# Casting the state powers to bf16 by transfers that GpSimd begins, with a new order of all steps, in a gated mix of attention and a state-space convolution

## The chip, the core and the metric

The kernel runs on one core of a Trainium2 chip. The metric is the device time of one execution in microseconds (us); smaller is better. The core's engines run side by side and meet at semaphores: PE (TensorE) multiplies matrices into PSUM, ACT (ScalarE) and DVE (VectorE) do the elementwise work and copy results out of PSUM ("evictions"), GpSimd (POOL) and SP (SyncE) begin transfers. Each engine runs its instructions strictly in the order in which they were written, so an instruction that waits holds up all that stand behind it on its engine.

## What is computed

Over 2048 tokens of width 512 the result is a gated sum of two branches, `g*a + (1-g)*b` with `g` a sigmoid of a weighted row sum of the input. Branch `a` is attention with 32 heads in four segments of 512 tokens, with a memory carried from segment to segment. Branch `b` is a state-space layer: each of the 512 channels has 128 complex states, whose powers give a long filter `K`, and the input is convolved with it.

```python
logdA = dt * A                                          # 512 x 128, complex
P = jnp.exp(logdA[:, :, None] * l[None, None, :])       # powers, l = 0 .. 2047 (rounded to bf16)
K = jnp.einsum('dn,dnl,dn->dl', Cc, P, dB).real
...
y = irfft(rfft(u padded) * rfft(K padded))[:L] + u * Dskip
...
return g * a + (1 - g) * b
```

## The kernel before

**How the order comes about.** `build_graph` makes a list of some 1800 steps, each with an engine, what it reads and writes, and a function that issues its instruction. Most evictions (`evac`, L223 to L229) and the cast of the powers are steps of the kind "ANY": they may run on ACT or on DVE. `ORDER` is a long text that a search outside the kernel has found; each word is a step's number, an `a` or `v` that puts a free step on ACT or DVE, and the buffer slots that it takes. `replay` reads it and so fixes the order on every engine; `emit` writes the instructions engine by engine and adds the semaphore waits that the data ask for. Transfers take their semaphores from a ring of 120 (`NDMA`): the 121st waits for the first to have landed. When SP has issued its last transfer it waits for all 120 in a row (L330 to L332).

**The stages.** To about 12 us parameters are loaded and transposed. The branches then run interleaved. *Attention*: for each of 4 segments and 4 head groups there are projections (L972 to L995), scores with an exponential of 128x2048 on ACT (L1062), masks (L1074), products with the values, and normalisations (L1034 to L1037). *Filter*: the states are squared nine times (below), tables of powers are multiplied up out of the results (L1157, L1160, L1164, all on DVE, for four blocks `c` of 128 channels), and PE correlates the tables ("lag" steps) into the filter. *Convolution*: two halves of 16 steps each, from about 130 us on, in which PE makes a spectrum X of the input, one K of the filter, DVE multiplies them (Y, L1266), PE turns the product back (V), and transfers on SP's queue load constants (`c_DNM`) and move parts. A last run on PE joins both branches and the output leaves in eight transfers.

**The state powers.** The channels are in two halves `h`. `Z` is an f32 tile of 128x512, 256 columns of real parts and 256 of imaginary parts. `ssm_powers` (L778) makes ten powers per half: ACT squares `Z` (L788), DVE makes the next `Z` of it (L789, L790). Of every `Z` a bf16 tile `pw` is made for the tables, in which each block of 128 channels has four strips of 128 columns: real, real again, imaginary, minus imaginary. For it there are three steps:

```python
# L796 on ACT or L797 on DVE: real and imaginary, cast to bf16
src = lambda Z=Z: ap(Z, 0, [[128, 2], [256, 2], [1, 128]])
dst = lambda pw=pw: ap(pw, 0, [[512, 2], [256, 2], [1, 128]])
# L798 on DVE: minus imaginary;  L800 on DVE: real again
```

So there are 20 casts (15 of them on DVE, 5 on ACT in this order), 20 negations and 20 copies. Table step `c` uses power 0 to 3 first, as copies into the table, and then all ten as factors; half 0 feeds blocks 0 and 1, half 1 feeds blocks 2 and 3. A table step waits for the whole `pw` of its power. GpSimd has only five memsets (L862, L914) and begins no transfer; SP begins all 263.

Of the kernel before, what the change touches and what calls it, by code (L numbers as in the profile page):

```python
# [7 lines left out]
ACT = mybir.ActivationFunctionType  # L8
# [4 lines left out]
NDMA = 120  # L13
# [80 lines left out]
class Op:  # L94
    __slots__ = ("eng", "cost", "fn", "deps", "key", "tiles", "wt", "seq", "alld", "tag", "alts", "isdma",
                 "idx", "inc", "val", "sem", "know", "waits", "pos")


class Sched:
# [61 lines left out]
    def op(self, eng, cost, fn, r=(), w=(), pw=(), key=None, acq=(), alts=None, isdma=False):  # L161
        o = Op()
        o.alts = alts
        o.isdma = isdma
        o.eng, o.cost, o.fn = eng, cost, fn
# [97 lines left out]
    def emit(self):  # L263
        nc, es = self.nc, self.es
        sems = {e: es.enter_context(nc.semaphore("q_" + e)) for e in ("PE", "ACT", "DVE", "POOL")}
        dsem = [es.enter_context(nc.semaphore("d%d" % i)) for i in range(NDMA)]
        block = es.enter_context(nc.Block())
        duse = [None] * NDMA
        dcnt = [0] * NDMA
        nd = 0  # L270
        last = {e: {} for e in self.prog}
        for o in self.order:
            know = dict(last[o.eng])
            o.waits = []
            deps = {id(d): d for d in o.alld}
            if o.isdma:
                k = nd % NDMA
                nd += 1
                if duse[k] is not None:
                    deps[id(duse[k])] = duse[k]  # L280
                duse[k] = o
                dcnt[k] += 1
                o.sem, o.val = ("D", k), dcnt[k]
            else:
                o.sem, o.val = o.eng, o.idx
# [28 lines left out]
        def make(e):  # L314
            def run(eng):
                for o in self.prog[e]:
                    need = {}
                    for d in o.waits:
                        s, v = tok(d)
# [9 lines left out]
                if e == "SP":  # L329
                    for k in range(NDMA):  # L330
                        if dcnt[k]:
                            eng.wait_ge(dsem[k], 16 * dcnt[k])  # L332
# [27 lines left out]
205/1 9/0 15/0 29/0 10/2 0/0 23/4/1 24v 54/0 1/0 57/1 30/11 38/5 33/9 21/0 39/0 14/1 31/2 17/0 34 35 36 32/6 45/1 37/7  # L360
44/12 58v/0 11/3 40/4 41 12/0 42 46/3 55/6 43 50/10 48/2 49/8 25/3/0 47 56v 51/1 52/0 61/3 3/0 59/0 60 16/0 53 62v/9
73/5 26a 178/1 74a/1 200/0/0/2 203/4/2 71/1 65/2 13/4 27/2/2 201a 72 173/7 202 63 85/4 83/3 84 18/0 20/0 204a 219/0/0
220 214/1/0/0 189/0 95/0 66/6 28v 67 250/3/2/0 174/1 96/0 98v/0 79/2 7/0 799/0 1247/1 208/2 221 97 64 86v/2 176/2 215
209a 99 109/3 190 87 175/0 240/0/1 241 588/0 1226/0 107/3 206/0 210/2 242 177 77/0 207a 994v/0 110v/3 75 181/1 179/2
76 191 111 108 88 228/0/2 251a 229 377/0 995v 122v/4 121/4 217 196/0 212/3 230 213v 119/3 78 197/0 223/0/3 224
1250/3/0 211a 89/0 120 123 998v/0 100 996v 192/0 225 253/2/0 1000/1 252 997v 254a 1002 222/0 999 1003/0 1001 124 1005
1004 236/0/0 237 134a/8 91/5 112 216 131/3 1232/2/1 226 135 1008 238 132/3 1233v 133 296/1/1 1011 1009/0 227 198/0
1248/2 1006/1 262/0/3 263 90 1249a 146v/5 231 6/0 1251a 235/2 199/0 232/0 1010 800/3 801 264 1234/3 136 147 145/7 233
1015/0 22/0 1252 234/1 103/0 101/3 1014 102 1235a 143/0 266/0/2 144 267 1016 1227/0/0 1007 1017 1012/0 158v/7 297a
193/0 148 1229/3 239 243 255/1/1/1 268 1230a 271/0/0 272 159 1236 113/3 1228a 273 378/3 244 293/0/1/1 279/0/1 280 1026  # L370
245/1 114/4 1231 294a 379 115 246 1013 391/0 247 1018/1 256 337/3/2 265/0 257 281 1242/2/1 1243a 1244/1 1245a 283/0/3
160 284 1246 1027/0 1019 269 270 274 589/2 155/0 285 157/1 156 295 218/1/0 125/3 802 380 275/2 1021/1 338a 307/0/2 308
127/3 590 258 1258/2/0 278/3 282 2/0 309 259 1020 1029 1259a 167a/6 592/0 276 1028 312/0/0 313 1022 1260/2 286 314 287
168 277/0 260/0 169 1239/0/1 248/1 1261a 288/2 1023 1240a 4/0 1024/0 1025 1030/1 303/0/1 304 126 1032 289 249a/0 305
334/0/0/2 1033/0 290 1034 139/7 335a 320/0/3 321 1035 1036/0 1031 298/2/0/1 137/0 306/0 310 339/1/1/0 1037 1237/3 311
315 322 1262 324/0/1 325 382/1 1238a 340 316/5 336 1043/3/0 1044 1045 341 1268/0 1265/1/0 138 299 300 317 151/1 326
318/1 182 1046 1241 301 194 1047v 149/0 291/2 346/0/2 292a 1266a 347 348 1038/2 1263/0 150 195 342 1039 1040 1041
1056v/0 1052v/0 1264a 319/1 1255/3/1 1061/1 350/0/0 351 383/0/2/0 323 327 328 1256a 161/1 1253/3 352 1055v 140v/9
355/0/3 1042a 1053v 1060 1054v 1289/1 1058/0 356 1057 386/2/0 1062 1254a 384a 1059 1066 1070/0 128v/0 398/3 1067/1 357
329/5 1063 349/0 1267 363/0/2 364 387a 353 1068 1069 1072 1048/0 8/0 385 330 399a 1071 92a/1 1073/1 1257 1064/0 1074  # L380
354 358 986/1 331 1079/1 1075 1065 359/4 1078 302/2 343 365 400/1/0/0 360 1080 344 401 443/3/1 361/0 402 93 1082/0
1081 367/0/1 1076/1 1083 444a 68a/4 368 1276/3/0 396/2 369 1274/1 405/0/0 1277a 1275a 1278 406 407 362/0 366 392/1
393a 397a 370 1284/3/1 1084 104v/3 129 1285a 371 409/0/3 410 1290/1/0 1292/2 1286/3 411 1293a 1077 372/5 1091/0 1085/1
1090 373 94 1086 374 1092 422/0/2 423 1087 445/1 1291a 1093 1094/0 1088/1 1095 1089 1294 394/2 390/1 440/1/1/1 424 261
395a 426/0/1 427 408/0 441a 1287a 442 116v/6 375/2 163/3 1271/1/0 412 162 446 170v/2 1288 490/3/0/2 428 1272a 413 491a
388/0 414/0/0 415 180 492 80v/7 152v/8 171 1101/1/1 1102 1103 1104 1269/3 416 459/0/3 376a 1105a 460 417 117 69 81 141
1281/2/1 421/1 105 425 429 430 164v/5 389 345 70 431/0 106 165 1270a 1279/3 418/3 432 1273 1049 1050 461 166 1282a
455/0/0 142 419 130 456 1096/2 1097 1098 1099 82 1280a 457 403 420/0 1302/3/0 1303a 433 118 448/0/1/1 449 153 1114v/0
1113v/0 1110v 1112v 1119/0 472/0/2 473 1300/1 1118 1111v 1116/1 1115 493/3/2 1283 1120 1117 474 1301a 1124 1121
464/0/1 1100a 465 1125/0 1128/1 450 1127 172 1126 1129 458/2 494a 1297/1/1 651/0/2/0 1295/3 462 463 1131/0 1304 466  # L390
476/0/0 1298a 1296a 477 652a 467 1307/1/0 471/3 475 332/0 478 520/0/3 1308a 521 1122/1 1130 1123 333a 1136 1132 468/3
522 1305/1 609/0/1 610a 1306a 512/0/2 1134/1 803 1137/0 381 513 469 1138 1133 434/0/2/0 470/1 1135 447/0 154 514
538/2/1/1 539a 479 503/0/1 504 541/2/0 505 451 480 495/0 1140/1 591 524/0/0 542a 435 1139 1106 1051 1323/0 436 1109
525 1141 1143/0 1148 540 481/3 437 484/0/5/1 482 1149/1 483 526 519/2 1309 1107 1299 1390/2 523 1108 1142 597/3/1 485
1150 486 507/0/3 1152/1 487 508 438/0 598a 1144 543/1 488/3 404/1/1 527 528 509 1145 1146/0 553/0/0 554 452 489a/0
439a 1151 602 506/3 510 511 453 546/0/1/1 529/0 515 1147 1310/1 530 1153 555 516/3 1337/1 1325/1 1326/1/2 547 653
531/0 496 1327a 1329 557/0/2 558 559 1328 1324/0 517 548 518 497/1 601/0 1154/1/0 1155 454 1156 549 593/0 498/0/0/0
# [1004 lines left out]
```

## Time and profile before

| | |
|---|---|
| median of 3 runs (lowest to highest) | 314.16 us (313.31 to 314.18) |
| the profiled execution, device time | 315.1 us |
| its span, first to last instruction | 313.3 us |
| mean granted clock of PE | 0.971 |
| busy: PE, DVE, ACT, GpSimd | 260.0, 264.3, 260.3, 3.2 us |
| chain of waits: DVE, PE, ACT, transfers | 31%, 30%, 20%, 9% |

The profile is one execution, recorded by the hardware. Its page gives busy times by engine, the span in 40 slices, transfers by queue, and groups of instructions: a line of the kernel, engine and operation, what is written and read, shape and number, then busy time, the mean duration of one in ns, and idle time of the engine before them with what ended it. "Busy time by stretches" gives the same for stretches of time. The "chain of waits" goes back from the last instruction, at each step to what released it or to the instruction before it on its engine; its pieces are given as start, length, engine and line. An engine's instructions overlap a little at their ends, so what one costs its engine is the distance from its start to the next one's start, not its duration.

### The profile page before, as it was taken

What the parts mean: (1) busy time and instruction counts of PE and PEld (TensorE: products, weight loads), DVE (VectorE), ACT (ScalarE), POOL (GpSimd) and SP (SyncE); (2) the same over time, 40 slices, a digit from 0 to 9 for tenths busy, and PEclk for the clock granted to TensorE, in tenths of its full rate; (3) what the DMA queues carried; (4) which work ended last, traced back from release to release, by engine and by line L of the source; (5) the groups of instructions that cost most, each with busy time, mean ns of one, the idle gap of its engine ahead of it and who ended that gap; (6) DMA issues with size and microseconds to landing.
All of it is one profiled execution on the core that took longest, in us unless ns stands there. A gap on an engine that the chain in (4) does not pass through costs nothing.

```text
span 313.3 us, 10366 instructions
## 1 busy us (share of the span) xinstructions
PE 260.0 (83%) x4393; PEld 183.1 (58%) x4430; DVE 264.3 (84%) x667; ACT 260.3 (83%) x315; POOL 3.2 (1%) x9
## 2 busy tenths in 40 slices
PE   1587688669977777989888899999999998999992
PEld 1343445345544543666546677667757775799892
DVE  1999999987999999999999768778999899883432
ACT  2899999997999999999999787988998998823250
POOL 2000000000000000000000000000000000000000
PEclk9999958996999999999999999999999999999999
DMA  5994111130402213431437676767668757873333
GB/s 148 273 235 84 35 68 50 36 104 10 144 33 71 79 47 106 108 97 25 130 112 237 191 216 180 228 187 254 204 191 245 249 164 238 242 250 91 109 112 100
DMA packets 49486, 44.51 MB, mean 142 GB/s; under 512 B 17184, under 2 KB 44832, under 8 KB 49440
## 3 DMA queue, kind: packets, MB, share of 16 engines
q1 hardware_dynamic: 49440, 43.85, 47.6%
q8 instruction: 35, 0.57, 0.8%
q14 instruction: 11, 0.09, 0.1%
HBM read 26.92 MB, written 6.29 MB: 106 GB/s over the span
## 4 chain that ended last, share of the span: by engine, by line
DVE 31%; PE 30%; ACT 20%; DMA 9%; issue 4%; SPq 4%; ACTq 0%; DVEq 0%
PE psum L680 29%; ACT sb L1062 9%; DVE sb L1157 7%; DMA sb<-c_DNM 7%; ACT sb L225 6%; DVE sb L1164 6%; DVE sb L1160 6%; SPq L221 4%; DVE sb L226 3%; ACT sb L788 2%; DMA sb<-sb 1%; DVE sb L1037 1%; DMA sb<-c_ident 1%; DVE sb L1266 1%; DVE sb L1034 1%
## 5 line engine op out<-in xcount | busy, mean ns | idle before, releaser
L680 PE MATMUL psum<-sb 128*128 128x17 bf16 (+12 forms) x4305 | 252.4, 224 | 39.1 <-ACT sb L1062 18.7
L680 PEld LDWEIGHTS psum<-sb 128*128 128x128 bf16 (+2 forms) x4342 | 176.6, 97 | 114.4 <-ACT sb L1062 32.2
L1062 ACT ACTIVATE sb<-psum 128x2048 bf16<-128x2048 f32 x80 | 152.4, 1905 | 5.4 <-PE psum L680 4.6
L225 ACT ACTIVATE sb<-psum 128x512 bf16<-128x512 f32 (+2 forms) x151 | 86.9, 627 | 25.4 <-PE psum L680 18.5
L226 DVE CAST sb<-psum 128x512 bf16<-128x512 f32 (+1 forms) x50 | 33.1, 677 | 5.1 <-PE psum L680 4.6
L1157 DVE TENSOR_TENSOR sb<-sb 128x512 bf16<-128x512 bf16 (+3 forms) x52 | 33.7, 663 | 0.0
L1164 DVE TENSOR_TENSOR sb<-sb 128x512 bf16<-128x512 bf16 (+3 forms) x52 | 33.5, 663 | 0.0
L1160 DVE TENSOR_TENSOR sb<-sb 128x512 bf16<-128x512 bf16 (+3 forms) x52 | 33.2, 656 | 0.0
L1266 DVE TENSOR_TENSOR sb<-sb 128x1024 bf16<-128x1024 bf16 x32 | 21.8, 688 | 6.9 <-DMA sb<-sb 5.5
L1074 DVE TENSOR_TENSOR sb<-sb 128x1024 bf16<-128x1024 bf16 (+1 forms) x40 | 22.8, 581 | 2.7 <-ACT sb L1062 2.7
L229 DVE TENSOR_SCALAR sb<-psum,sb 128x256 bf16<-128x256 f32 x18 | 8.5, 482 | 14.2 <-PE psum L680 9.4
L1037 DVE TENSOR_TENSOR sb<-psum,sb 128x256 bf16<-128x256 f32 x32 | 13.3, 420 | 0.6 <-PE psum L680 0.3
L228 ACT ACTIVATE sb<-psum,sb 128x256 bf16<-128x256 f32 x14 | 6.1, 473 | 6.8 <-PE psum L680 5.9
L788 ACT ACTIVATE sb<-sb 128x512 f32<-128x512 f32 x18 | 11.7, 653 | 0.0
L1034 DVE RECIPROCAL sb<-psum 128x16 f32<-128x16 f32 x32 | 8.1, 252 | 2.2 <-PE psum L680 2.1
L736 PE MATMUL psum<-sb 128*128 128x128 bf16 x24 | 3.1, 311 | 7.4 <-DMA sb<-c_ident 5.8
L226 DVE COPY sb<-psum 128x1024 bf16<-128x1024 bf16 x4 | 2.7, 686 | 6.8 <-PE psum L736 6.8
L1114 DVE TENSOR_TENSOR sb<-psum,sb 128x512 bf16<-128x512 f32 x12 | 8.2, 682 | 0.2
L993 ACT ACTIVATE sb<-sb 128x512 bf16<-128x512 bf16 x12 | 7.8, 652 | 0.0
L790 DVE SCALAR_TENSOR_TENSOR sb<-sb 128x256 f32<-128x256 f32 x18 | 7.4, 417 | 0.0
L789 DVE TENSOR_TENSOR sb<-sb 128x256 f32<-128x256 f32 x18 | 7.3, 414 | 0.1
L736 PEld LDWEIGHTS psum<-sb 128*128 128x128 bf16 x24 | 2.5, 144 | 8.2 <-DMA sb<-c_ident 5.8
(67 smaller groups left out, 109.7 us busy)
## 6 DMA issues: line engine op xcount, KB each, us to landing
sb<-c_DNM SPq DMA_DIRECT2D x32, 320.0 KB, 3.7
sb<-c_DNM SPq DMA_DIRECT2D x32, 192.0 KB, 3.1
scr_Z<-sb SPq DMA_DIRECT2D x16, 256.0 KB, 2.6
sb<-scr_Z SPq DMA_DIRECT2D x32, 128.0 KB, 3.0
sb<-sb SPq DMA_DIRECT2D x64, 64.0 KB, 3.2
sb<-sb SPq DMA_DIRECT2D x32, 128.0 KB
sb<-in_A_x_dram SPq DMA_DIRECT2D x5, 512.0 KB, 4.5
out_dram<-sb SPq DMA_DIRECT2D x8, 256.0 KB, 2.2
```

The lines of the kernel that those rows point to most:

```text
L221: return self.op(q, ("D", nbytes), lambda e: e.dma_start(out(), in_(), **kw), r=r, w=w, pw=pw, key=key, isdma=True)
L225: fa = lambda e: e.activation(dst(), src(), ACT.Copy)
L226: fd = lambda e: e.tensor_copy(dst(), src())
L680: mm = lambda e, o_, l, r_, st, sp, **kw: e.matmul(o_, lhsT=l, rhs=r_, start=st, stop=sp, skip_group_check=True, **kw)
L788: op("ACT", ("As", 512), lambda e, sq=sq, Z=Z: e.activation(ap(sq, n=512), ap(Z, n=512), ACT.Square), r=[Z], w=[sq], key=PW[h] + PWS * k)
L1037: op("DVE", ("V1", 256), lambda e: e.tensor_tensor(ap(o1, gi * 16, [[128, 4], [32, 4], [1, 16]]), ap(T, dims=[[68, 4], [17, 4], [1, 16]]), ...
L1062: o = op("ACT", ("Ax", 2048), lambda e, P=P, pT=pT: e.activation(ap(pT, n=2048), ap(P, n=2048), ACT.Exp, scale=0.25), r=[P], w=[pT])
L1074: op("DVE", ("V2", 128 * nb), lambda e, pT=pT, dims=dims: e.tensor_tensor(ap(pT, dims=dims + [[1, 128]]), ap(pT, dims=dims + [[1, 128]]), ...
L1157: op("DVE", ("V2", 256 * n), lambda e: e.tensor_tensor(run(tile, ne, dst, 1), run(tile, ne, src, sstep), ap(pw, cl * 512, [[2, 128], [0, n ...
L1160: op("DVE", ("V2", 256 * n), lambda e: e.tensor_tensor(run(t2, n, 0, 1), run(tile, ne, src, sstep), ap(pw, cl * 512 + 256, [[2, 128], [0, ...
L1164: op("DVE", ("V2", 256 * n), lambda e: e.tensor_tensor(D_(), D_(), ap(t2, n * 128, [[-n * 128, 2], [2 * n, 64], [1, 2 * n]]), ALU.add), r= ...
L1266: op("DVE", ("V2", 1024), lambda e, Y=Y, XAB=XAB, K3=K3: e.tensor_tensor(ap(Y, dims=[[512, 2], [1, 512]]), ap(XAB, dims=[[512, 2], [1, 512 ...
```

## The change

The cast, which was one step on ACT or DVE, becomes three transfers that GpSimd begins; they read `Z` in f32 and write `pw` in bf16. The first writes the imaginary strips, the second the real ones, the third the real ones again. The copy on DVE is gone. The negation stays on DVE and reads what the first transfer wrote.

```diff
-                op("ANY", 0, None, r=[Z], pw=[pw], key=PW[h] + PWS * k + 0.3, alts={
-                    "ACT": (("As", 512), lambda e, dst=dst, src=src: e.activation(dst(), src(), ACT.Copy)),
-                    "DVE": (("Vs2", 512), lambda e, dst=dst, src=src: e.tensor_copy(dst(), src()))})
+                pp = [pw.part() for _ in range(3)]
+                for i, (d0, z0) in enumerate(((256, 256), (0, 0), (128, 0))):
+                    S.dma(lambda pw=pw, d0=d0: ap(pw, d0, [[512, 2], [1, 128]]), lambda Z=Z, z0=z0: ap(Z, z0, [[128, 2], [1, 128]]), 65536,
+                          r=[Z], w=[pp[i]], pw=[pw], key=PW[h] + PWS * k + 0.3, q="POOL")
                 op("DVE", ("V4", 256), lambda e, pw=pw: e.tensor_scalar(
-                    ap(pw, 384, [[512, 2], [1, 128]]), ap(pw, 256, [[512, 2], [1, 128]]), -1.0, None, ALU.mult), r=[pw], pw=[pw], key=PW[h] + PWS * k + 0.4)
-                op("DVE", ("V4", 256), lambda e, pw=pw: e.tensor_copy(
-                    ap(pw, 128, [[512, 2], [1, 128]]), ap(pw, 0, [[512, 2], [1, 128]])), r=[pw], pw=[pw], key=PW[h] + PWS * k + 0.4)
+                    ap(pw, 384, [[512, 2], [1, 128]]), ap(pw, 256, [[512, 2], [1, 128]]), -1.0, None, ALU.mult), r=[pp[0]], pw=[pw], key=PW[h] + PWS * k + 0.4)
```

The semaphores of transfers grow from 120 to 150: GpSimd's 60 transfers get one each and SP's share the other 90.

```diff
-NDMA = 120
+NDMA = 150
...
+        npool = sum(o.isdma for o in self.prog["POOL"])
+        nhw = NDMA - npool if npool > 20 else NDMA - 30
+        dsem = [es.enter_context(nc.semaphore("d%d" % i)) for i in range(nhw + npool)]
...
-                k = nd % NDMA
-                nd += 1
+                if o.eng == "POOL":
+                    k = nhw + nsw
+                    nsw += 1
+                else:
+                    k = nd % nhw
+                    nd += 1
...
-                    for k in range(NDMA):
+                    for k in range(len(dsem)):
```

`ORDER` is replaced as a whole: 1818 steps in place of 1798, in another order on every engine, with other evictions on ACT and DVE and other buffer slots. In the new text GpSimd's queue holds two memsets first, then the casts of half 0 with the third memset after the eighth of them, then the casts of half 1, and the memsets of the last two segments behind all casts. A mark `tr` on transposing loads is added and is not used by the kernel itself.

## The prediction, made before the run

> **What bounds the kernel now.** I read the page's busy shares first, then the busy time by stretches, then the chain of waits, and last the ends of the queues.
>
> ```profile
> PE 260.0 (83%) x4393; PEld 183.1 (58%) x4430; DVE 264.3 (84%) x667; ACT 260.3 (83%) x315; POOL 3.2 (1%) x9
> ```
>
> Three engines are level and GpSimd is empty, so an average names no bound. The stretches do (columns: PE, weight loads, DVE, ACT, GpSimd, clock, DMA):
>
> ```profile
> 20.00:40.00 20.00, 14.44 (x182) 7.75 (x184) 19.91 (x72) 19.66 (x26) 0.00 (x0) 0.98 0.41 90
> 80.00:100.00 20.00, 16.59 (x226) 9.34 (x229) 20.00 (x40) 20.00 (x26) 0.66 (x1) 1.00 0.24 82
> 120.00:140.00 20.00, 16.96 (x445) 11.88 (x440) 19.96 (x51) 19.10 (x23) 0.00 (x0) 1.00 0.37 105
> 180.00:200.00 20.00, 18.83 (x247) 14.44 (x248) 14.59 (x39) 16.53 (x23) 0.00 (x0) 1.00 0.68 202
> 280.00:313.30 33.30, 27.08 (x275) 24.67 (x273) 11.78 (x24) 9.23 (x20) 0.00 (x0) 0.98 0.37 110
> ```
>
> From 20 to 140 us (and on to about 170) DVE and ACT are both full; afterwards PE is the fullest, and at the end it is alone. The chain of waits agrees: it runs through ACT from 13 to 70 us, through DVE from 77 to 157, then mostly through PE's L680. All that the change removes lies before 121 us, inside the full stretch. The same chain gives prices, since its pieces run from start to start:
>
> ```profile
> 14.67 0.52 ACT sb L796
> ...
> 22.02 0.49 ACT sb L225
> ...
> 33.98 0.61 DVE sb L226
> ...
> 102.77 0.67 DVE sb L797 x2
> 103.44 0.81 DVE sb L798 x6
> ```
>
> So a cast on DVE costs 0.67/2 = 0.335 us of the engine, not the 0.421 of its group's mean (the tails overlap); a 256-wide bf16 operation 0.81/6 = 0.135; a cast on ACT 0.52; an eviction of 512 columns 0.49 on ACT and 0.61 on DVE.
>
> **What goes.**
>
> ```profile
> L797 DVE CAST sb<-sb 128x512 bf16<-128x512 f32 x15 | 6.2, 421 | 0.0
> L800 DVE COPY sb<-sb 128x256 bf16<-128x256 bf16 x20 | 4.1, 211 | 0.0
> L796 ACT ACTIVATE sb<-sb 128x512 bf16<-128x512 f32 x5 | 3.3, 661 | 0.0
> ```
>
> DVE loses 15 x 0.335 = 5.0 and 20 x 0.135 = 2.7, together 7.7 us (L800 priced as L798: same shape, 211 and 213 ns). ACT loses 5 x 0.52 = 2.6. The 20 negations stay.
>
> **What moves.** Reading the engine letters of both orders: five 512-wide evictions go from ACT to DVE (ACT -5 x 0.49 = -2.4, DVE +3.0) and some small ones go the other way (about ACT +1.4, DVE -1.1). In all DVE has 5.8 us less and ACT 3.6, mean 4.7. Counted ahead of the same step in both orders at the same prices, DVE has 2.7 and ACT 6.2 us less ahead of the Y product of the first half's step 4 (172 us now), and DVE 4.0 and ACT 4.4 less ahead of the second half's last Y product (287.7 us now). DVE is the later of the two at the first place, so the full stretch should end between 2.7 and 4.4 us earlier; by the last Y product both agree on about 4. I take -4.0, with ends at -2.7 and -5.8 (all that DVE loses). PE's work is the same set, and its last uncovered run (15.2 us after 292.6) keeps its length.
>
> **What is added at the end.** The last output transfer is issued here:
>
> ```profile
> 302.88 6.36 SPq L221 DMA_DIRECT2D out_dram<-sb  x5
> ```
>
> It is issued by 309.2 and lands at 311.0 (the trace's landing record), yet the span ends at 313.3. The records of SP's semaphore instructions show why: from 309.28 to 312.88 it works through the final list of 120 waits in 60 instructions, 0.060 us each, all of them long fulfilled. The list, not the transfer, ends the kernel. With 150 semaphores it has 15 instructions more: +0.9 us. Nothing hides this, since SP reaches the list only after its last issue. That the 263 transfers of SP now share 90 semaphores in place of 120 means up to 30 more waits in SP's queue, for transfers 90 issues old and long landed; at 0.03 each, spread over the kernel, I set it to nothing (ends 0 and +0.9).
>
> **What is added at GpSimd.** Sixty transfers of 64 KB in place of the casts. No row of this trace has a transfer begun by GpSimd, so two quantities are bounded: the pace g at which it begins one after another, and the landing. The nearest row for the landing is SP's:
>
> ```profile
> sb<-sb SPq DMA_DIRECT2D x64, 64.0 KB, 3.2
> ```
>
> I take 3.2 us from beginning to landing (lower end 2.2, the output's). For g the low end is SP's own issue, 0.6 in the chain; the high end is 3.2, if each had to land before the next began. The nearest rows of GpSimd itself are its memsets, 0.65 and 0.86 us; I take 0.9. The DMA engines are busy 0.41 of 20 to 40 us and 0.24 of 80 to 100, so the bytes fit.
>
> Does that come in time? In the new order half 0's powers are needed much sooner: power 9 first enters a table product where DVE has 37.3 us of work ahead of it; DVE runs full with 7.1 us of idle before (in the trace of before, 16.5 us of work stand ahead of the first table copy, at 23.6), so at 44.4 us, where now it is 57.2. Its last transfer is the 27th of GpSimd's queue. The first can begin at 13.8, when L770 ends. Landing of the n-th is 13.8 + (n-1)g + 3.2. The 27th is in time if g is at most (44.4-17.0)/26 = 1.05; the 25th (power 8, needed at 41.5) and the 22nd (power 4, 38.4) give 1.02. At 0.9 nothing waits. Half 1's casts are not tight: they are needed from 97 us on and can mostly begin by 70. Two memsets of the value tiles now stand behind all casts on GpSimd; they ran at 89.3 and 151.5 us, and the first reader of segment 2's comes at about 165 us, so these wait for nobody. Each negation now waits for a landing, and behind it on DVE stands everything: a late landing is paid in full by a full engine.
>
> **Sum.** Against the profiled execution (span 313.3, 315.1 us with 1.8 us around it): 315.1 - 4.0 + 0.9 = 312.0. That execution is 0.9 above the median of 314.16, so 311.1 on the median's scale; the times below are on that scale. A measurement here can tell about 0.3%: faster is below 313.2, slower above 315.1.
>
> **Rivals.**
>
> *GpSimd's pace (slower).* Place: half 0, 13.8 to 50 us. DVE stops at power 4, then 8 and 9, whose lateness adds up to that of the worst. At g = 1.2 the 25th is 4.3 us late: 315.4. At 1.4 the 27th is 9.0 late: 320.1. At 1.6, 14.2: 325.3. At 3.2, 55.8: 366.9. It decides from g = 1.02, and at 1.02 + 3/24 = 1.15 the gain is gone. For it: three needs in a row sit within 0.03 us of the same pace, so there is no slack, and g was chosen from memsets. Against: SP issues in 0.6. I give 0.18 to a pace of 1.05 to 1.25 (centre 1.15, about 314) and 0.14 to more.
>
> By the Trainium skill (DMA: Bandwidth & Descriptors, "Anatomy of one DMA — SWDGE (gpsimd) path") a transfer from GpSimd has a fixed part of about 2.0 us, most of it the write receipt and not the generation. If that part were paid one after another, the same formula would give 13.8 + 26 x 2.0 + 3.2 - 44.4 = 24.6 us of lateness and 335.7; by the page it overlaps. No row here shows it.
>
> *GpSimd holds up DVE (slower).* DVE's operations with one source in SBUF are its fast ones here (0.335 us for 512 f32 columns against 0.61 from PSUM; 0.135 for 256 of bf16). If these wait while GpSimd prepares a transfer, 33 of them (17 negations, the rest L984, L944, L994, L995 and table copies) lie in the two stretches in which the casts are begun; at half a pace each, 33 x 0.45 = 14.9 us, so 326.0. In the trace of before GpSimd is idle after 2.4 us but for two memsets, so nothing there speaks for it; against the full price speaks that in half 1 the 30 casts fill only 27 of some 40 us. Chance 0.12.
>
> The Trainium skill (SBUF — State Buffer, "Who interferes with whom") states such a rule: VectorE's two-port modes and GpSimd share one port pair as an exclusive lock, held for the whole instruction, and whichever comes second blocks; elsewhere on the page it tells the case with GpSimd's descriptors starved by VectorE, which would lengthen g instead, by at most the 2.8 us that 18 such operations take in half 0.
>
> *The gain does not reach the end.* The tail from 172 us is PE, loads of c_DNM and SP's issues in the chain; if these start no earlier because a transfer or a buffer sets them, only the longer list remains: 314.16 + 0.9 = 315.1. For it: the whole order is new, and a shorter DVE in front of a PE-bound tail is no shorter tail. Against: the tail's first steps wait for the tables that DVE makes (in the chain L1164 stands before PE's correlations at 137 us). Chance 0.14.
>
> **How the numbers follow.** Forecast 0.42, at 311.1; its own range 309.3 (-5.8) to 312.4 (-2.7). Pace slightly over 0.18 (faster 0.05, same 0.08, slower 0.05). Pace well over 0.14 and the held-up DVE 0.12, both slower. No gain at the end 0.14 (same 0.06, slower 0.08). Together faster 0.47, same 0.14, slower 0.39. The range goes from 309.0 to 326.0: it takes in the forecast's low end, the pace to 1.6 and the held-up DVE at half a pace; left out are slower paces (about 0.07) and part of the last rival.
>
> **What would show it.** Right: L797, L800 and L796 gone; DVE full from 20 to 140 with no idle before the negations and none put down to a transfer; power 9's table product near 44 us; the last Y product near 284; 75 wait instructions at SP's end. Wrong: DVE idle between 33 and 52 us, ended by a transfer (pace); negations or L984 far longer than 0.22 and 0.35 us while GpSimd works (held up); the last Y product still at 288 with DVE ahead of time at 140 (no gain). The forecast stands on g: it falls with any pace above 1.15.

## The result, and the profile after

The changed kernel takes 325.5 us (median; 323.92 to 327.57) beside 314.14 for the kernel before in the same rounds: ratio 1.0372, 95% interval [1.0295, 1.0449], slower by 11.7 us. Forecast were 311.1. The profiled execution took 327.57 us, its span 325.8, at a granted clock of 0.930 (before 0.971). All ratios here leave out runs more than 1.5% above the fastest of the same kernel (five of e2's ten), the medians do not, so where both stand side by side the sums go by the ratios, times 314.1 us.

The page's busy times after:

```profile
PE 272.2 (84%) x4430; PEld 185.3 (57%) x4430; DVE 262.6 (81%) x633; ACT 258.8 (79%) x309; POOL 45.7 (14%) x69
```

DVE has 34 instructions less and yet only 1.7 us less busy time; PE, whose work is the same set, has about 12 us more (of its 4430 products the trace of before lacks 37). The busy time by stretches (columns: PE, weight loads, DVE, ACT, GpSimd, clock, DMA share, GB/s):

```profile
20.00:40.00 20.00, 16.26 (x226) 9.02 (x225) 18.27 (x62) 18.57 (x26) 11.11 (x17) 0.85 1.44 182
80.00:100.00 20.00, 17.55 (x239) 10.22 (x237) 17.89 (x33) 18.54 (x23) 14.49 (x21) 0.95 0.80 106
120.00:140.00 20.00, 16.22 (x360) 10.71 (x356) 19.80 (x43) 17.88 (x17) 0.00 (x0) 1.00 0.26 74
180.00:200.00 20.00, 17.28 (x222) 13.32 (x222) 13.62 (x38) 14.95 (x24) 0.00 (x0) 1.00 0.66 200
280.00:325.80 45.80, 37.46 (x462) 33.45 (x458) 20.33 (x47) 17.52 (x29) 0.00 (x0) 0.95 0.40 119
```

Where GpSimd begins transfers (20 to 40, 80 to 100) DVE and ACT are no longer full: 18.27 and 17.89 where 19.91 and 20.00 stood. The work went, and the time stayed. What DVE waits for between 14 and 172 us, the first four lines (in total, times, longest):

```profile
DVE sb L969 <- PE psum L688: 1.9, 1, 1.9
DVE sb L1039 <- PE psum L688: 1.2, 1, 1.2
DVE sb L798 <- DMA sb<-sb: 0.9, 1, 0.9
DVE sb L805 <- DMA sb<-sb: 0.4, 1, 0.4
```

Only 1.3 us are waits for transfers: 0.4 by a negation (L805), and 0.9 by L798, the next state, which needs a `Z` slot that a cast still reads. The other waits are for PE (3.3 us) and ACT (0.9); in all they are 5.5 us, in before 3.8. The transfers themselves, from the page's groups and its DMA issues, and the beginning of GpSimd's timeline (start, length):

```profile
L222 POOL DMA_DIRECT2D sb<-sb x60 | 42.8, 718 | 62.8 <-DVE sb L227 26.1
...
sb<-sb POOLq DMA_DIRECT2D x60, 64.0 KB, 3.6
```

```profile
13.32 2.25 POOL L222 DMA_DIRECT2D sb<-sb  x3 [11.48 <-DVE sb L778]
16.54 3.62 POOL L222 DMA_DIRECT2D sb<-sb  x5 [0.97 <-DVE sb L797]
20.15 0.68 POOL L919 MEMSET sb<- 128x128 bf16 x1
20.40 5.86 POOL L222 DMA_DIRECT2D sb<-sb  x8
```

Eight in 5.86 us are 0.73 each, and 3.6 us pass from issue to landing. The pace is better than the 0.9 that the prediction took.

The 3.6 us are a median, and it hides the beginning. By the landing records the first 16 transfers, begun between 13.3 and 25.5 us, landed 3.9 to 10.2 us later, where the prediction took 3.2 for each. The negation that waits 0.4 us waits for one that was begun at 18.73 and landed 8.2 us later. The DMA share of 20 to 40 us is 1.44, where the prediction read 0.41 in before and concluded that the bytes fit. A transposing load that SP began at 18.3 us landed 14.7 us later (5.8 in before). Little of this is waited for, though: DVE's waits for transfers are the 1.3 us above, PE's 0.2.

**Place by place.** The same step compared in both traces: at 107 us the changed kernel is 1.0 behind, at the product Y of the first half's step 4 it is 2.9 behind (175.0 against 172.1; forecast 2.7 to 4.4 ahead), at the second half's step 4 11.2 behind, at the second half's last Y product 9.8 behind (297.5 against 287.7; forecast about 4 ahead), and the last output transfer is issued at 318.7 against 308.9. From there to the end of the span pass 7.1 us, before 4.4.

### The profile page after: what moved, and what is told of

It reads as the page before. It is cut to its first block, busy times and chain, and to the rows that moved or that the text cites. A ratio compares the mean times of both kernels' runs of the same rounds, so it can differ in the third digit from the quotient of the medians.

```text
span 325.8 us, 10455 instructions
## 1 busy us (share of the span) xinstructions
PE 272.2 (84%) x4430; PEld 185.3 (57%) x4430; DVE 262.6 (81%) x633; ACT 258.8 (79%) x309; POOL 45.7 (14%) x69
## 4 chain that ended last, share of the span: by engine, by line
PE 35%; DVE 28%; DMA 13%; ACT 10%; issue 7%; POOL 3%; SPq 2%; DVEq 0%
PE psum L688 34%; DMA sb<-sb 8%; ACT sb L1067 6%; DVE sb L1162 4%; DVE sb L1169 4%; DVE sb L1165 4%; DVE sb L227 4%; DMA sb<-c_DNM 3%; ACT sb L226 3%; POOL sb L222 2%; SPq L222 2%; DVE sb L1271 2%; DVE sb L1079 2%; DMA sb<-c_ident 1%; DVE sb L1042 1%
## 5 line engine op out<-in xcount | busy, mean ns | idle before, releaser
L688 PE MATMUL psum<-sb 128*128 128x17 bf16 (+10 forms) x4342 | 266.1, 228 | 38.0 <-ACT sb L1067 12.3
L688 PEld LDWEIGHTS psum<-sb 128*128 128x128 bf16 (+3 forms) x4342 | 178.8, 98 | 122.9 <-issue 34.9
L226 ACT ACTIVATE sb<-psum 128x512 bf16<-128x512 f32 (+2 forms) x147 | 83.0, 608 | 26.8 <-PE psum L688 26.5
L222 POOL DMA_DIRECT2D sb<-sb x60 | 42.8, 718 | 62.8 <-DVE sb L227 26.1
L227 DVE CAST sb<-psum 128x512 bf16<-128x512 f32 (+1 forms) x54 | 36.5, 681 | 13.1 <-PE psum L688 12.7
L230 DVE TENSOR_SCALAR sb<-psum,sb 128x256 bf16<-128x256 f32 x17 | 7.6, 481 | 12.9 <-PE psum L688 6.6
L229 ACT ACTIVATE sb<-psum,sb 128x256 bf16<-128x256 f32 x15 | 6.8, 473 | 12.0 <-DVE sb L230 8.1
L1042 DVE TENSOR_TENSOR sb<-psum,sb 128x256 bf16<-128x256 f32 x32 | 13.3, 418 | 0.3
L919 POOL MEMSET sb<- 128x128 bf16 x4 | 2.7, 664 | 48.8 <-PE psum L688 48.5
L798 DVE SCALAR_TENSOR_TENSOR sb<-sb 128x256 f32<-128x256 f32 x18 | 7.5, 415 | 1.0 <-DMA sb<-sb 0.9
```

The source lines that it names most:

```text
L222: return self.op(q, ("D", nbytes), lambda e: e.dma_start(out(), in_(), **kw), r=r, w=w, pw=pw, key=key, isdma=True)
L226: fa = lambda e: e.activation(dst(), src(), ACT.Copy)
L227: fd = lambda e: e.tensor_copy(dst(), src())
L688: mm = lambda e, o_, l, r_, st, sp, **kw: e.matmul(o_, lhsT=l, rhs=r_, start=st, stop=sp, skip_group_check=True, **kw)
L1042: op("DVE", ("V1", 256), lambda e: e.tensor_tensor(ap(o1, gi * 16, [[128, 4], [32, 4], [1, 16]]), ap(T, dims=[[68, 4], [17, 4], [1, 16]]), ...
```

## The experiments

Each ratio is to the kernel before, run on the same chip. First theory: the new order itself makes the kernel late. Its rival: the transfers do.

**e1, e2, e3: order and casts taken apart.** e1 takes the graph of before (casts and copies on the engines) in the order of after. e2 and e3 keep the new graph:

```diff
 e2, in the changed kernel
-                    S.dma(... pw ..., ... Z ..., 65536, r=[Z], w=[pp[i]], pw=[pw], ..., q="POOL")
+                    op("POOL", ("G", 256), lambda e, ...: e.memset(ap(pw, d0, [[512, 2], [1, 128]]), 0.5),
+                       r=[Z], w=[pp[i]], pw=[pw], ...)
 e3: the changed kernel with ORDER = that of before, casts as early as Z and the slot allow,
     negation just ahead of its first reader, no copies
```

> The new order with the casts and copies back on ACT and DVE (5 and 15, as before the change, each at the place where its first transfer stood; the copy behind the negation), 120 semaphores. If the new order itself is the slow part (theory), the time stays at 324 to 330: the transfers are gone, and 10.3 us of work come back on two engines. If the transfers are the slow part (rival: their landings, their descriptors, or GpSimd holding up DVE), it falls to 314 to 319.

> The new kernel with each of the 60 casting transfers replaced by a GpSimd memset of the same part of the same tile (the powers are then a constant; the cast is left out), everything else in the same order. Memsets took 0.65 us on GpSimd, the transfers 0.71, but nothing is moved and nothing lands late. Order theory: 323 to 326. Rival: the transfers' traffic and landings cost most of the 11 us, so 314 to 318.

> The old order with the casts as GpSimd's transfers, each begun as soon as its state and its buffer are there, the negation just ahead of the first reader, the copy gone; 150 semaphores. Order theory: the full stretch sheds 4 us and the list at the end costs 0.9, so 310 to 313. Rival: the transfers slow this order as well, 318 to 326.

| | median us | ratio, 95% interval |
|---|---|---|
| e1 new order, casts on engines | 326.2 | 1.0396 [1.0323, 1.0468] |
| e2 new order, memsets for the casts | 319.0 | 1.0098 [1.0048, 1.0147] |
| e3 old order, GpSimd's casts | 323.8 | 1.0332 [1.0256, 1.0408] |

e1 lies where the order theory had it, e3 where its rival had it, and e2 outside both of its ranges. Neither theory holds alone. With the casts nearly free (e2) the new order is still 3.1 us slower than before by the ratio (its ten executions lie between 315.0 and 320.8 us, and the mean of all ten would make it 4.0), and the transfers cost in the old order too (e3). In e3 DVE waits 4.2 us for transfers, twice, both times with the next state that needs a `Z` slot.

**e4, e11: the end.** SP's final list is cut to the semaphores of the output transfers, in the kernel before (e4) and in the changed one (e11).

```diff
-                        if dcnt[k]:
+                        if dcnt[k] and duse[k].tag.startswith("fir"):
                             eng.wait_ge(dsem[k], 16 * dcnt[k])
```

> The kernel before, but SP's list at the end waits for the output transfers alone. In the trace the list runs from 309.28 to 312.88 us and the last output lands at 311.03. If the list sets the end, 1.8 us go: 312.3. If something else follows that takes its place (rival), 314.1.

> The changed kernel, in which SP's final list holds only the semaphores of the eight output transfers. In every kernel so far with GpSimd's transfers the span ends 7.1 us after the last output transfer is issued, in all others 4.4, in e4 with the short list 2.7. If this end is a cost of its own: 325.5 less 4.4, 320 to 322.5. Rival, that the list costs only its 15 more instructions as forecast (0.9) beside the 1.4 that e4 gained: 323 to 324.

e4: 312.7, ratio 0.9944 [0.9901, 0.9987]. e11: 320.4, ratio 1.0175 [1.0112, 1.0238], so 5 to 6 us less than after, and its span ends 2.7 us after the last output's issue, like that of e4. The end is a price of its own, and larger than forecast. The timeline of SP in after has the last issues:

```profile
311.19 7.88 SPq L222 DMA_DIRECT2D out_dram<-sb  x7
```

The records of SP's semaphore instructions behind it: 75 in place of 60, at 0.06 us, as forecast, two semaphores in each. But the eighth of them waits until 2.2 us after the last issue: in it stands the semaphore of that very output. The records show that SP does not begin with the first semaphore but in the middle of the numbers, in after with number 76, in before with 61. SP's 263 transfers share 90 semaphores in after, so the last one has number 263 - 2 x 90 = 83, and that is in the eighth instruction; the other 67 come after the landing, where in before most of them covered it. In before the ring has 120, the last output's semaphore has number 263 - 2 x 120 = 23 and stands in the 39th of the 60 instructions, which SP reaches after the landing.

**e5, e7, e8: what the transfers cost if nobody waits for them.** e5 is e3 with e2's memsets. In e7 and e8 GpSimd begins 60 transfers of the same shape from a constant tile to one that nobody reads:

```diff
+    for n, (h, k) in enumerate(IDLE):
+        q = n % 4
+        o = S.dma(lambda q=q: ap(iddT, q // 2 * 512 + q % 2 * 128, [[256, 2], [1, 128]]),
+                  lambda: ap(idsT, 0, [[128, 2], [1, 128]]), 65536, r=[idsT], w=[iddp[q]], q="POOL")
+        o.deps += [z for z in idz[(h, k)] if z not in o.deps]
```

> The order of before, with a GpSimd memset in place of each of the 60 casting transfers of e3 (the cast itself is left out, so the powers' bf16 tiles hold a constant); the negations stay, semaphores 150. If what costs 10 us in e3 (323.8) is waiting for the transfers, or the transfers themselves, it is gone here and the 7.7 us of DVE work saved may show: 308 to 313. Rival, that an order made for casts on the engines can use no free cast, or that the longer GpSimd queue and list cost the time: 316 to 323.

> The kernel before, casts on the engines as they were, and 60 casting transfers of GpSimd of the same shape and size besides, at the places of e3, from a constant tile to one that nothing reads; no engine waits for them; 150 semaphores. If the transfers themselves (descriptors, the DMA engines, the ports) slow the other engines: 318 to 323. Rival, that only waiting for their landing costs: 313.8 plus 0.9 for the longer list, 314 to 316.

> e2 (the new order with memsets in place of the casts, so the cast is left out; 319.0) and 60 casting transfers besides, one behind each memset in GpSimd's queue, from a constant tile to one that nothing reads; no engine waits for them. If the transfers themselves cost the 6.5 us between e2 and after: 323 to 327. Rival, that waiting for their landing costs it: 318 to 320.5.

e5: 317.7, 1.0119 [1.0065, 1.0173], slower than before although nothing is cast; that is its rival's time, but the rival's reason stayed open until e18. Beside it, e3 and e5 have the same order on every engine and differ in that memsets stand for the transfers: 6.7 us (1.0332 against 1.0119), 2.7 of them the end and 4.0 the rest, e3's waits for transfers included. e7: 319.7, 1.0189 [1.0132, 1.0246]. e8: 325.1, 1.0329 [1.0262, 1.0396]. e7 and e8 lie where the theory of the transfers themselves had them: transfers that nobody waits for add 5.9 us to before, 2.7 of them the end, 3.2 the rest; in the new order, on top of e2, 7.2 and 4.5 (there one wait of 1.3 us for a memset that stands behind transfers in GpSimd's queue). What DVE's short operations make of it; before, the negation and the scaling of a 512-column tile:

```profile
L984 DVE TENSOR_SCALAR sb<-sb 128x512 bf16<-128x512 bf16 x16 | 5.3, 336 | 0.0
L798 DVE TENSOR_SCALAR sb<-sb 128x256 bf16<-128x256 bf16 x20 | 3.9, 213 | 0.0
```

e7, negation and copy (the copy took 211 before):

```profile
L814 DVE TENSOR_SCALAR sb<-sb 128x256 bf16<-128x256 bf16 x20 | 5.4, 288 | 0.0
L816 DVE COPY sb<-sb 128x256 bf16<-128x256 bf16 x20 | 4.5, 248 | 0.0
```

After, the same two as in before:

```profile
L989 DVE TENSOR_SCALAR sb<-sb 128x512 bf16<-128x512 bf16 x16 | 5.9, 367 | 0.5 <-ACT sb L226 0.4
L805 DVE TENSOR_SCALAR sb<-sb 128x256 bf16<-128x256 bf16 x20 | 5.3, 287 | 0.4 <-DMA sb<-sb 0.4
```

In e7 this is 20 x 0.075 + 20 x 0.037 = 2.2 us of a full DVE. DVE is held up while GpSimd prepares transfers, as the second rival had it, at a seventh of its price. That these 2.2 us make up most of the 3.2 is not shown: in e7's trace the steps are 1.0 us behind before at 107 us and 0.5 at 172, and in e17 (below) DVE's casts are held up by half as much with no loss that shows.

**e6, e12: the halved clock.** PE's clock line of after and, below, of e6:

```profile
PEclk9899578786999979999999999999989989999996
```

```profile
PEclk9999869999999999989999899999999999999996
```

After loses 41.0 us of its first 300 to windows at half clock (37.5 without one at 13.6 us), before 17.1. A theory that this is the cause: e6 and e12 keep PE busy with products of the identity that nobody reads, e6 164 of them in 35 places, e12 68 in 19. Shown are those that are issued ahead of the step's own wait; the others stand behind it.

```diff
+                    b, c = WARM.get(n, (0, 0)) if e == "PE" else (0, 0)
+                    if b > 0:
+                        for _ in range(c):
+                            eng.matmul(self.ap(self.bank, b * 512 + 288, n=128), lhsT=self.ap(self.identT, n=128),
+                                       rhs=self.ap(self.identT, n=128), start=False, stop=True, skip_group_check=True)
 ...
```

> The changed kernel, in which PE multiplies the identity by itself 164 times more (0.056 us each at the full clock, 9 us in all) into columns of PSUM that nothing reads or that the next product overwrites, in 35 places between 25 and 131 us where its trace shows PE streaming few rows. In the traces so far the granted clock is halved in a 3.4 us window when in the window before PE streamed less than about 0.36 of its rows and columns; after lost 37.5 us to halved windows, before 17.0. If the halved clock is what makes the changed kernel late, these windows fall to 15 us or less up to 135 us and the time to 316 to 321. Rival, that the halved clock is only a sign of PE waiting and costs nothing: the clock rises and the time stays at 325 or goes up to 333 with the added work.

> As e6, with 68 idle products in 19 places instead of 164 in 35 (3.8 us at the full clock instead of 9.2), put only where the trace of the changed kernel shows windows under 0.42. In e6 the halved windows fell from 34.1 us to 6.8 before 135 us and the time did not fall, but the added work may have eaten the gain. If the halved clock is a price of its own: 317 to 321. If PE waits less at the halved clock and nothing else is gained: 323 to 327.

e6: 327.9, 1.0449 [1.0368, 1.0530], with 13.7 us of halved windows. e12: 326.3, 1.0356 [1.0278, 1.0434], with 23.9. Two thirds and two fifths of the halved windows are gone, and the time is not better. The added work (9.2 and 3.8 us at the full clock) may hide a small gain; as the main cause the halved clock falls. Why clearing its windows gains nothing is not shown. It is not that PE has time to spare in them: in after PE is busy for 39 of the 41 us that these windows take.

**e9, e10, e13 to e16: what work is worth in the full stretch.** If DVE sets the pace, work taken off it must show. Kernels with about 5 us less work before 140 us (of the old order but for e10), which leave parts of the computation out as the expectations say:

```diff
 e9 (casts and copies on both engines), e10 (the same in e1), e13 (those on DVE alone)
-    ... ap(pw, 0, [[512, 2], [256, 2], [1, 128]]) ... ap(Z, 0, [[128, 2], [256, 2], [1, 128]])
+    ... ap(pw, 0, [[512, 2], [256, 2], [1, 2]]) ... ap(Z, 0, [[128, 2], [256, 2], [1, 2]])
 e14
-    e.activation(ap(pT, n=2048), ap(P, n=2048), ACT.Exp, scale=0.25)
+    n=(1280 if 0 < 4 * s + hg < 8 and ti == 4 else 2048): e.activation(ap(pT, n=n), ap(P, n=n), ...)
 e15, the projections
-                for k in range(4):
+                for k in range(3 if s < 2 else 4):
 e16: e13, e14 and e15
```

> The kernel before with its order, in which the 20 casts and the 20 copies keep their places and waits but write 2 columns of each strip instead of 128 (so most of the powers' bf16 tiles hold a constant that one GpSimd memset writes at the start); GpSimd does nothing else new and the list has 120 semaphores. It prices what the change could save at most in the old order. If DVE's work up to 170 us sets the time, as the prediction had it: 7.7 us less less some 2 for the small operations, 307.5 to 310. Rival, that PE and ACT, full beside DVE, take over at once: 312 to 315.

> e1 (the new order, casts on the engines at the places where the changed kernel begins its transfers; 326.2) with the same 2-column casts and copies as e9, so most of the powers' tiles hold a constant. No GpSimd work beside one memset at the start, list of 120. If the new order is late in itself, through its tail (21.2 us from the last Y product to the last output against 17.2 before): 317 to 321, as e2 with its memsets. Rival, that e2's 319.0 still holds a price of the memsets on GpSimd and the order is as good as forecast: 309 to 313.

> The kernel before, in which the 15 casts on DVE and the 20 copies write 2 columns of each strip instead of 128 (most of the powers' tiles hold a constant that one DVE memset writes in DVE's idle time ahead of 6.8 us). About 5 us less DVE work between 14 and 121 us, the same on ACT and PE. Theory of the prediction, that the full DVE sets the pace: 309 to 311. Theory now, that DVE, ACT and PE hand the pace to each other and none sets it alone: 312 to 314.5.

> The kernel before, in which 7 of the 80 exponentials (the last one of head groups 1 to 7, before 135 us) take 1280 of their 2048 columns; the rest of those scores keeps old values. About 5 us less ACT work, the same on DVE and PE. If ACT sets the pace: 309 to 311. If none does alone: 312 to 314.5.

> The kernel before, in which the projections of the first two segments add up three of their four products (24 products of 512 columns left out, 0.216 us each at the full clock): about 5.2 us less PE work before 135 us, the same on DVE and ACT. If PE sets the pace, with its waits for the exponentials and its halved windows: 309 to 311. If none does alone: 312 to 314.5.

> e13, e14 and e15 together: about 5 us less on each of DVE, ACT and PE before 135 us, with the same parts left out. If the three hand the pace to each other, work off all of them shows in full: 308.5 to 310.5, and the gains of the three single kernels add up to less than this one's. If one engine sets the pace alone, this is as fast as that one's kernel.

| | less work | ratio, 95% interval | us against before | own start | left |
|---|---|---|---|---|---|
| e9 | DVE 5.0, ACT 2.2 | 1.0072 [1.0017, 1.0127] | +2.3 | +2.2 | +0.1 |
| e13 | DVE 5 | 1.0111 [1.0039, 1.0184] | +3.5 | +4.6 | -1.1 |
| e14 | ACT 5 | 1.0013 [0.9978, 1.0048] | +0.4 | 0 | +0.4 |
| e15 | PE 5 | 0.9965 [0.9921, 1.0010] | -1.1 | 0 | -1.1 |
| e16 | all three | 1.0013 [0.9968, 1.0058] | +0.4 | +4.6 | -4.2 |

"Own start" is a side effect of these kernels: the memset that fills the powers' tiles delays DVE's first steps (in e13 and e16 it ran from 2.94 to 11.53, where DVE had its first eviction at 6.83; in e9 see the last section). The steps behind it carry this lag in the trace (e13 is 4.5 us behind at 35 us, 5.4 at 140), so it is taken off; with it in their times e9, e13 and e16 lie above the ranges of their expectations. The intervals are 1.1 to 2.3 us wide to each side, so e9 and e13 to e15 say "little or nothing", not their exact size. The stretch from 20 to 140 us, in before and in e13:

```profile
20.00:140.00 120.00, 94.17 (x1961) 58.71 (x1982) 116.75 (x325) 115.36 (x140) 0.66 (x1) 0.93 0.27 76
```

```profile
20.00:140.00 120.00, 95.78 (x1759) 58.71 (x1784) 111.70 (x316) 115.01 (x143) 0.67 (x1) 0.89 0.25 71
```

DVE's busy time fell by 5.05 us, and the place at 140 us came no earlier once the late start is taken off: the 5 us became waits (DVE waits 8.1 us between 14 and 172 us, in before 3.8). With less work on all three, e16 goes from 4.4 us behind at 35 us to 0.4 behind at 140, and by the ratios it is 3.1 us faster than e13, which has the same late start. e14 and e15 are 1.1 and 2.3 us ahead at 140 in their traces, but e4, where nothing is changed there, is 1.9 ahead too, so these traces cannot tell a gain of that size. No kernel here takes work off ACT and PE without DVE, so whether DVE's share counts in e16 is open. e10 (327.2, 1.0381 [1.0310, 1.0451], 2.8 of it its start) is as slow as e1 and outside both of its ranges: there casts stand in ACT's and DVE's queues where the new order has GpSimd begin transfers, ACT waits 11.9 us for PE before 170 us (5.4 in before), and neither kernel says how good the order is for what it was made for. That is left to e2.

**e17, e18: GpSimd's work, or the place of small operations.** e5 had remained unexplained. e17 is e7 with unused memsets in place of the transfers; e18 is e5 with each negation at its old place in DVE's order, which then is that of before without the casts and copies.

```diff
 e17
+        o = op("POOL", ("G", 256), lambda e, q=q: e.memset(ap(iddT, ...), 0.5), r=[idsT], w=[iddp[q]])
 e18: ORDER, negation where before has it, in place of just ahead of the first reader of its power
```

> The kernel before, casts on the engines as they were, and 60 GpSimd memsets of 256 bf16 columns besides, at the places of e7's idle transfers, into a tile that nothing reads. If GpSimd's work beside the others is what makes e5 and e2 late (it holds DVE up: in e9 a tensor_scalar of 0.29 us took 2.29 beside a long memset): 316 to 319. If not: 313.5 to 315.

> e5 (memsets in place of the casts, which are left out) with each negation at its old place in DVE's order instead of just ahead of its first reader; DVE's and ACT's orders are those of before without casts and copies. If the moved negations make e5 late: 312.5 to 314.5. If GpSimd's work does: 316 to 318.5.

e17: 315.6, 1.0015 [0.9977, 1.0053]: short memsets on GpSimd cost nothing that shows, though DVE's casts beside them take 491 ns in place of 421 (the time lies just above the range of that expectation):

```profile
L813 DVE CAST sb<-sb 128x512 bf16<-128x512 f32 x15 | 7.3, 491 | 0.0
```

e18: 314.1 beside 315.2 for before in its rounds, 0.9937 [0.9895, 0.9980]: faster by 2.0 us. e5 and e18 do the same work on every engine and differ in the places of 20 operations of some 0.25 us each; that is worth 5.7 us (1.0119 against 0.9937, with intervals 1.3 to 1.7 us wide to each side). The stretch from 20 to 140 us in e18, and its largest group of DVE's waits between 14 and 172 us:

```profile
20.00:140.00 120.00, 97.65 (x2044) 59.30 (x2042) 111.19 (x291) 113.82 (x136) 16.11 (x51) 0.93 0.27 76
```

```profile
DVE sb L227 <- PE psum L687: 6.2, 4, 3.3
```

and the same of before:

```profile
DVE sb L226 <- PE psum L680: 3.0, 2, 2.3
```

With 5.6 us less on DVE and 1.5 on ACT the trace of e18 is 0.7 us ahead of before at 167 us. DVE now waits 8.7 us for others, before 3.8.

## Why the prediction was wrong, point by point

The forecast is 311.1, the result 325.5. By ratios the 11.7 us divide into three terms, the forecast's own:

| term | forecast | measured | from |
|---|---|---|---|
| less work and the new order | -4.0 | +3.1 | e2 |
| transfers beside the rest | 0 | +5.9 | after less e2 less the end |
| the end | +0.9 | +2.7 | 7.1 against 4.4 us in the traces; e11 |

The split of the first two rows hangs on e2 and is uncertain by some 2 us (its interval is 1.6 us wide to each side), and part of the second row belongs to the order and is no price of the transfers (see "The order").

**The failed step: "DVE is the later one at the first place, so the full stretch should end between 2.7 and 4.4 us earlier".** The prices of what went hold roughly (in e18 DVE is 5.6 us less busy between 20 and 140; 1.3 of what lacks to 7.7 are negations that take 277 ns there in place of 213). So does the count of the work ahead of both marks. The inference from them, that the stretch ends earlier by the work that the fuller engine loses, does not. e2, whose casts are nearly free, has the new order's work and nothing late, and reached the first mark 1.5 us earlier than before (170.6 against 172.1; forecast 2.7 to 4.4) and the last Y product 0.2 earlier (287.4 against 287.7; forecast about 4), in its fastest execution.

Five us off DVE alone gained 1.1 +- 2.3, off ACT nothing, off PE 1.1 +- 1.4, off all three 4.2 +- 1.4. Even with the old order and the casts free of cost (e18) 7.7 us of DVE's work and 2.6 of ACT's were worth 2.0. An explanation that fits is that the engines hand the pace round: in before, between 14 and 170 us, DVE (97% busy from 20 to 140) waits 3.8 us, mostly for PE, ACT (96%) waits 5.6, mostly for PE, and PE (78%) waits 17.9 for exponentials. It is not proven: the single gains add up to 1.8 with a margin of some 3, which does not exclude the 4.2 of all three.

**The order.** That leaves 5.1 us (3.1 + 2.0) between e18 and e2, which differ in the order. I treated two orders with the same steps as equal but for the sums of work ahead of a step. e5 against e18 shows what that misses: the places of 20 small operations alone are worth 5.7. Which places of the new order cost its 5.1 was not tried.

The traces show where the new order loses. Take the stretch from the first half's step 4 (172.1 us in before) to the second half's last Y product (287.7), in which no cast runs. In it after, e1, e2, e6, e8, e10, e11 and e12 lose 7.0, 4.4, 1.3, 6.8, 7.7, 6.4, 7.4 and 1.8 us against before; the kernels of the old order lie between 1.7 less and 1.8 more. e1 and e10 begin no transfer on GpSimd, so this loss goes with the order, and the 5.9 us in the table hold a part of it. DVE's evictions wait for PE there (172 to 246 us), in the new order for 7.1 to 11.7 us, in the old one for 1.2 to 3.8. Before, then e1:

```profile
DVE sb L226 <- PE psum L680: 2.7, 5, 0.8
```

```profile
DVE sb L226 <- PE psum L679: 10.9, 8, 6.1
```

e2 has these waits too (10.5 us) and loses only 1.3 in its trace, so they mark the order and do not measure its price. What makes the loss 1.3 in one kernel's trace and 7.7 in another's is open.

**"Its last uncovered run keeps its length".** This held. The prediction's mark is the second half's last Y product: 287.7 us in before, 287.4 in e2, 297.5 in after. From there to the issue of the last output 21.2 us pass in all three. What failed is that no gain reached the mark. In the chain of waits PE's last piece is longer in e2 and seems to say otherwise; e2:

```profile
285.97 21.59 PE psum L688 x219
```

and before:

```profile
292.58 15.22 PE psum L680 x152
```

These pieces begin elsewhere in the work. The Y product that is last in time is another step in before (at 291.7 us) than in e2 (287.4): the new order draws it forward, so 29 of PE's steps stand behind the last one in place of 24. Comparing the last in time would show a gain of 4.3 us that is none.

**The end.** The count (15 instructions, 0.9 us) was right. Missed was that the ring of 90 puts the last output's semaphore near the place where SP begins the list: another 1.8 us.

**The pace (rival).** Refuted: 0.73 us, where it would have decided from 1.02. Power 9's first table product stood at 47.2 us (forecast 44.4, before 57.2); DVE waited 0.4 us with a negation. The landing in the same formula was mis-sized, 3.9 to 10.2 us for the first 16 transfers in place of 3.2, and it cost no more than these waits.

**GpSimd holds up DVE (rival).** It does, for some 2 us in place of 14.9; that its 326.0 lies near the 325.5 measured is a coincidence. It takes no transfer to hold DVE up: in e18, where GpSimd has memsets only, negations take 277 ns. In after they take 287 ns in place of 213 on average, the longest 744, the median 218: most pass freely. The Trainium skill (SBUF — State Buffer, "Who interferes with whom") says that the second of the two fully blocks for the whole of the first one's instruction; the long memset of the last section agrees (2.29 us in place of 0.29), and so do the few negations that take up to 0.74.

**Not listed by me.** A cast holds its `Z` until it lands, and the next state waits for the slot: 0.9 us in after, 4.2 in e3. The rest of the 5.9 us is not divided further here: part of it is the loss behind 172 us that goes with the order. e2's profiled execution is its fastest, 314.97 us against a median of 319.0, so e2's small loss there is in part its luck.

**No gain at the end (rival).** Its mechanism, that a shorter DVE ahead of a PE-bound tail is no shorter tail, came closest. In e2 step 4 is 1.5 us ahead and the last Y product stands at 287.4, which is near the sign ("still at 288") that the prediction had named for it. But it was priced as if nothing else could get worse.

Of the kernels that compute everything, e4 is the best: before with the short list, 0.9944 [0.9901, 0.9987]. It beats both.

## What to carry to other kernels

Where two engines are 96% busy side by side, do not price work taken off one of them at its full length: take it off in a trial first, and off each engine that is full. A new order is a change of its own, even with the same steps: compare the same step in both orders, and not the last of its kind in time, and look for the stretches in which one order waits more than the other. And look where in the final list of waits the semaphore of the last transfer stands.

## What the hardware showed that I had not expected

**A long memset of GpSimd stops DVE's fast operations.** In e9's timeline DVE, then GpSimd:

```profile
7.91 0.42 DVE L755 TENSOR_TENSOR sb<-sb 128x256 f32<-128x256 bf16 x1
8.24 2.29 DVE L757 TENSOR_SCALAR sb<-sb 128x256 f32<-128x256 f32 x1
```

```profile
0.97 8.93 POOL L1353 MEMSET sb<- 128x10240 bf16 x1
```

The `tensor_scalar` takes 0.29 us in before. Here it ends at 10.53 us; the long memset's record ends at 9.90 and that of GpSimd's next memset at 10.40. The `tensor_tensor` ahead of it runs at its usual 0.42 beside the same memset. DVE's own memset of that size was no faster (8.59 us in e13).

**The halved clock goes with little streaming, not with idleness alone.** The clock records stand 3.41 us apart. I weighed each matmul's columns by the share of the 128 rows that it uses and summed them over these windows, as a share of what full streaming would be (512 columns in 0.216 us, the distance of such products in after where they follow each other at full clock). Over all 20 traces, from the first clock record to 300 us, of the windows at full clock with a share under 0.33, 52 of 56 were followed by one at half clock; of those from 0.33 to 0.40, 28 of 78; from 0.40 to 0.45, 1 of 77; above, none of 1314. PE was far from idle in many of them: products with 16 rows (the scores) or 17 columns (the values) fill its busy time and hardly count. The Trainium skill (TensorE: Matmul & The Clock Gate, Part 1) has the clock fall after an idle window; a window 80% busy in the page's sense was enough here (30.7 us in after, with a share of 0.18). What that costs is another matter (e6, e12).

**PE stops without a visible reason** once near 70 us in nearly every kernel, for 0.9 (e12) to 3.0 us (e11; 1.3 in before), in the middle of a step; in after a transfer of 16 KB on an instruction queue runs at that time (72.7 us). It was seen, and not tried.
